# A hand-ordered attention and expert kernel: two cleared tiles fall away, and three weight splits change places at the end of attention

## The chip, the cores and the metric

The kernel runs on one core of a Trainium2 chip. The metric is the device time of one execution in microseconds (us); lower is better. Five engines take part, each with a program of its own that it works off in order: TensorE (PE in the profile, with its weight loads as PEld), VectorE (DVE), ScalarE (ACT), GpSimd (POOL) and SyncE (SP, which here only issues DMAs). GpSimd issues the gathers and scatters, which are indirect DMAs.

## The reference, cut to what matters

```python
# attention: 8 batches x 8 heads x 576 tokens, head size 64; k and v are averaged over groups of 8 tokens
k_p = k.reshape(B, H, 72, 8, D).mean(axis=3);  v_p = v.reshape(B, H, 72, 8, D).mean(axis=3)
attn = softmax((1 / sqrt(D)) * q @ k_p^T)
x = attn @ v_p                      # rows of 512 values, one for each of 8 * 576 = 4608 tokens
# experts: 8 of them, 512 -> 1024 -> 512; each token goes to one
logits = x @ w_gate;  local = sigmoid(x @ w_local)
# in each batch, token by token:
e = argmax(logits[s]) if s == 0 or local[s] < 0.5 else the expert of the token before
out[s] = softmax(logits[s])[e] * (relu(x[s] @ w1[e]) @ w2[e])
```

## The kernel before

**Attention** runs in 20 units, five to each of four pairs of batches (units 0 to 4 are pair 0, 15 to 19 pair 3). A unit takes 128 rows of queries of one or two tokens each, makes scores (`sc`), their maximum and difference (`mx`, `sb`, VectorE) and exponentials (`ex`, ScalarE), transposes them (`T0`, `T1`, `T2` on TensorE; `T0c` to `T2c` copy the result out on ScalarE), multiplies with the values (`v0`, `v1`, `v2` on TensorE, line 568; `v0c` to `v2c` copy out into `osb` on ScalarE), and scales: `fr` makes the reciprocals `rr` (line 585, VectorE), `fs` scales and sums the logits (`lgx`, line 590, and `lg`, VectorE), `fp` and `fd` scale the rows `xs` (line 606; both halves on GpSimd, or one on VectorE after `.d`) and send them to `x_rows` in DRAM.

**Routing** follows each pair in the steps `rA` (lines 624 to 639, VectorE), `rT0` to `rT2` (transposes into the small PSUM tiles `tp`), `rS0` to `rS2` (scans, line 653, VectorE), `rE`, `rL`, `rO`, `rR`, `rV` (lines 687 to 693, VectorE) and `rP`. It ends in nine scatters (`s`, line 707, GpSimd), which write each token's number into the list of its expert, `ids`.

**Weights.** After pair 1 the kernel chooses the expert with the most tokens so far and loads its weights (`w1`, `w2`). A float32 weight is used as a high and a low part. `p1:c` and `p2:c` split a piece of 128x1024: ScalarE writes the high part, and then a second engine subtracts it from the raw weights, which gives the low part. With `.d` that engine is VectorE, without it GpSimd:

```python
def split2(src, c, eng):
    s = slice(2 * c, 2 * c + 2)
    nc.scalar.copy(out=W2[0][:, s, :], in_=src)
    eng.tensor_tensor(out=W2[1][:, s, :], in0=src, in1=W2[0][:, s, :].bitcast(F32), op=ALU.subtract)
```

**First blocks.** `il` loads the token numbers of a block of 256 tokens of that expert (`idm`). `ga` turns them to integers (`idr`, line 292, VectorE), clears the tile `qt` that the rows go to (line 261, GpSimd), and issues two gathers from `x_rows` (line 265). Both blocks hold tokens of pairs 0 and 1 alone; a list entry past these rows is left out by the gather's bound. `X0` and `X1` transpose the gathered rows on TensorE (line 277), `X0c` and `X1c` copy and split them (line 284 on ScalarE, line 285 on VectorE). `L1` is the first layer (lines 322 and 324), `h0` and `h1` its results' way out of PSUM (lines 329 to 335; `h0` on ScalarE and then VectorE, line 330), `L2` the second layer (line 349).

**Order.** Nothing is scheduled by a planner. Three lists of steps are written out by hand (`PLAN` for attention, `PLAN_B` for the first two blocks and the last routing, `PLAN_C` for what follows), and each step puts its instructions on its engines in the order of the list, so that the list is at once the order within every engine. A loop over the other blocks follows; in it TensorE is busy almost all the time. TensorE's products use PSUM tiles with few buffers: `tp` has two, `op` has two, `hp` has three; the routing's transposes and those of attention share `tp`. `vt_in` and `kt` hold raw weights (three and two buffers), `qt` has four buffers.

Of the kernel before, what the change touches and what calls it, by code (L numbers as in the profile page):

```python
# [78 lines left out]
vc:19 v2c:12 ch:0 vm.a:22 fr:12 v0:11 v0c:11 sb:14 vc:20 T0:13 lk:14 v1:11 T0c:13 s:0 s:0 v1c:11 T1:13 v2:11 rR:1 er:0  # L79
T2:13 rV:1 vm.a:18 s:0 sc:15 T1c:13 rP:1 ex:14 T2c:13 vl:19 lq:17 w2:1 fp:12 lq:18 lq:16 v2c:11 vt:18 kc:15 v0:13 fr:11  # L80
vm.a:19 T0:14 mx:15 vd:19 vc:18 T0c:14 s:0 fp:11 w1:3 vl:20 sb:15 vd:20 T1:14 vt:22 v1:13 w1:2 T1c:14 vc:22 vl:18
fd.p:12 s:0 fd:11 fs:11 lv:23 vd:18 vm.a:21 sc:17 fs:12 vt:21 s:0 kp:14 ex:15 s:0 s:0 v0c:13 p2:1 v1c:13 v2:13
s:0 mx:17 sb:17 vc:21 v2c:13 p1.d:3 T0:15 w2:0 v0:14 fr:13 T0c:15 lq:19 vl:21 s:0 T1:15 v0c:14 s:0 fp.d:13 kc:14 T2:15
T1c:15 v1:14 v0:15 fs:13 v1c:14 fd:13 sc:16 fr:14 vd:21 vp.d:23 w1:1 T2c:15 ex:17 s:0 p1:2 fs:14 T0:17 v0c:15 fp:14
w1:0 T1:17 v1:15 vl:22 T0c:17 mx:16 T1c:17 v2:15 fd.p:14 T2:17 v1c:15 sb:16 il:0 vt:23 v0:17 vm.a:23 rA:2 vc:23 T2c:17
sc:18 v2c:15 ex:16 fr:15 T0:16 vd:22 mx:18 rT0:2 vl:23 vd:23 rS0:2 v1:17 T0c:16 T1:16 v0c:17 sb:18 v2:17 fp:15 v1c:17
T1c:16 T2:16 rT1:2 fd.p:15 p2:0 ga:0 fs:15 p1.d:0 v2c:17 fr:17 fp:17 v0:16 rS1:2 T2c:16 sc:19 ex:18 rT2:2 mx:19 v0c:16
rS2:2 v1:16 v1c:16 v2:16 rE:2 sb:19 v2c:16 T0:18 T0c:18 T1:18 rL:2 T2:18 T1c:18 fr:16 fs:17 ex:19 il:1 fd.p:17 fp:16
rO:2 fd:16 v0:18 rR:2 ga:1 T2c:18 fs:16 p1.d:1 X0:0 v0c:18 X0c:0 T0:19 v1:18 v1c:18 T0c:19 v2:18 X1:0 v2c:18 T1:19
rV:2 v0:19 fr:18 X1c:0 T1c:19 v1:19 v0c:19 fs:18 v1c:19  # L90
""")
PLAN_B = plan("""
# [13 lines left out]
def moe_attention(ctx: ExitStack, tc: tile.TileContext, q, q_st, k, v, v_st, w_gate, w1, w2, out):  # L106
    nc = tc.nc
# [149 lines left out]

    def rows_gather(i, xg, rows=None):
        row_numbers(idrs[i], idms[i])
        if rows:  # L260
            nc.gpsimd.memset(xg, 0.0)
        for h in range(2):
            off = bass.IndirectOffsetOnAxis(ap=idrs[i][:, h:h + 1], axis=0)
            if rows:
                nc.gpsimd.indirect_dma_start(out=xg[:, h, :], out_offset=None, in_=x_rows[0:rows], in_offset=off,
                                             bounds_check=rows - 1, oob_is_err=False)
            else:
                nc.gpsimd.indirect_dma_start(out=xg[:, h, :], out_offset=None, in_=x_rows[0:NT + 1], in_offset=off)
# [22 lines left out]
    def row_numbers(out, m):  # L291
        nc.vector.tensor_copy(out=out, in_=m[:, :, 0])  # L292
# [60 lines left out]
    with ExitStack() as actx:  # L353
# [405 lines left out]
        qg, qT, kg, vg, sc, att, fin, rw, tr2, vl = {}, {}, {}, {}, {}, {}, {}, {}, {}, {}  # L759
        first1, first2, lgs, fr = {}, {}, {}, {}  # L760
        reg = {}

        xg = xt = xs = xq = sp = None
# [9 lines left out]
        def do(name, n):  # L773
# [86 lines left out]
            elif op == "ga":  # L860
                xgs[n] = ld.tile([P, 2, D], F32, name="qt", bufs=4)
                rows_gather(n, xgs[n], 4 * S)
            elif op in ("X0", "X1"):
                xtp[n, op] = rows_turn(int(op[1]), xgs[n])
# [38 lines left out]
            elif op == "g1":  # L903
                xgs["n"] = ld.tile([P, 2, D], F32, name="qt", bufs=4)
                rows_gather(NS, xgs["n"])
            elif op in ("Y0", "Y1"):
                xt = xts[NS - 1]
# [370 lines left out]
```

## Time and profile before

| | us |
|---|---|
| median of 3 runs | 612.84 |
| lowest, highest | 612.37, 613.87 |
| the profiled execution | 618.07 |
| its span, first to last instruction | 615.5 |

The profiled execution has its own time; it is 5.2 us above the median of the runs without a profile, and 2.6 us of it lie outside the span. In its rows a start is counted from the span's start. A row of a timeline gives start, duration, engine, line, operation, output and inputs with shape, how many instructions are merged in it, and in brackets how long the engine sat idle just before and what ended the wait.

### The profile page before, as it was taken

The page shows a single profiled execution, that of the slowest core. Times are in us where ns is not written, and L with a number is a line of the kernel's source. Part 1 is how long each engine was busy: PE and PEld are TensorE (multiplying, and loading weights), DVE is VectorE, ACT ScalarE, POOL GpSimd, SP SyncE. Part 2 cuts the span into 40 slices and gives each one's busy share as a digit, 9 for nine tenths or more (in the row PEclk, how much of TensorE's full clock was granted, in tenths as well). Part 3 has the DMA queues.
Part 4 walks back from the last instruction along what each step waited for, and adds up shares of the span by engine and source line. Part 5 has one row for each costly group of instructions (what it writes and reads, how often), then busy time and mean ns, then how long its engine had stood idle before and what let it go on. Part 6 is the DMA issues. An engine that isn't in the chain of part 4 may idle for free. (4 is left out here: it accounts for less than half of the span.)

```text
span 615.5 us, 14456 instructions
## 1 busy us (share of the span) xinstructions
PE 593.8 (96%) x3392; PEld 512.7 (83%) x3393; DVE 412.6 (67%) x976; ACT 318.5 (52%) x732; POOL 281.9 (46%) x524
## 2 busy tenths in 40 slices
PE   8999999998999999999999999999999999999991
PEld 7998988987878888888888888888888888888881
DVE  7998898998866433643893585798536585634680
ACT  2777777965433223433662474668334473433561
POOL 6596776766475234232243426154152332331351
PEclk9999999997999999999999999999999999999997
DMA  8998983975102763422483457487743275223313
GB/s 345 358 390 296 358 290 108 332 166 169 56 1 98 229 235 115 130 79 91 118 325 104 146 186 289 125 333 221 269 123 107 102 274 186 92 80 101 114 40 91
DMA packets 62272, 111.94 MB, mean 182 GB/s; under 512 B 13730, under 2 KB 34210, under 8 KB 62244
## 3 DMA queue, kind: packets, MB, share of 16 engines
q1 hardware_dynamic: 53732, 89.54, 43.4%
q0 software_dynamic: 8512, 22.07, 10.9%
q8 instruction: 13, 0.21, 0.2%
q14 instruction: 15, 0.12, 0.1%
HBM read 81.88 MB, written 31.80 MB: 185 GB/s over the span
## 5 line engine op out<-in xcount | busy, mean ns | idle before, releaser
L322 PE MATMUL hp<-x,w1h 128*128 128x512 f32 x364 | 130.6, 399 | 0.5 <-DVE x L316 0.4
L349 PE MATMUL o_ps<-w2h,ht_h 128*128 128x512 f32 x312 | 122.8, 393 | 0.0
L349 PE MATMUL o_ps<-w2l,ht_h 128*128 128x512 f32 x312 | 122.0, 391 | 0.6 <-DVE w2l L178 0.5
L324 PE MATMUL hp<-x,w1l 128*128 128x256 f32 x364 | 102.1, 281 | 0.0
L330 DVE TENSOR_TENSOR hs<-hp,hs 128x256 f32<-128x256 f32 x91 | 37.7, 421 | 80.1 <-ACT hs L329 70.7
L349 PE MATMUL o_ps<-w2h,ht_l 128*128 128x512 f32 x312 | 87.6, 390 | 0.0
L322 PEld LDWEIGHTS hp<-x,w1h 128*128 128x128 f32 x364 | 68.4, 188 | 17.7 <-issue 0.8
L1107 POOL TENSOR_TENSOR zf<-m_e,ob 128x1 f32<-128x1 f32 x42 | 15.7, 375 | 128.8 <-ACT ob L1095 76.3
L568 PE MATMUL op<-vaug,aT 128*128 128x148 f32 (+4 forms) x448 | 67.4, 310 | 2.2 <-ACT osb L370 2.1
L324 PEld LDWEIGHTS hp<-x,w1l 128*128 128x128 f32 x364 | 68.7, 189 | 0.8
L349 PEld LDWEIGHTS o_ps<-w2l,ht_h 128*128 128x128 f32 x312 | 58.6, 188 | 12.9 <-DVE w2l L178 1.5
L349 PEld LDWEIGHTS o_ps<-w2h,ht_l 128*128 128x128 f32 x312 | 58.6, 188 | 12.5
L349 PEld LDWEIGHTS o_ps<-w2h,ht_h 128*128 128x128 f32 x312 | 58.6, 188 | 12.4
L334 ACT ACTIVATE ht_h<-hs 128x256 fp32r<-128x256 f32 x136 | 57.1, 421 | 22.4 <-DVE hs L330 14.7
L329 ACT COPY hs<-hp 128x256 f32<-128x256 f32 x91 | 33.5, 370 | 64.6 <-PE hp L324 56.6
L568 PEld LDWEIGHTS op<-vaug,aT 128*128 128x128 f32 (+1 forms) x448 | 61.1, 181 | 6.0 <-ACT osb L370 3.1
L335 DVE SCALAR_TENSOR_TENSOR ht_l<-hs,ht_h 128x256 fp32r<-128x256 f32 x136 | 57.3, 423 | 5.9 <-ACT ht_h L334 5.4
L1095 ACT ACTIVATE ob<-o_ps,m_a 128x512 f32<-128x512 f32 x40 | 27.4, 685 | 54.9 <-PE o_ps L349 54.9
L1108 POOL DMA_INDIRECT out<-ob,m_e x42 | 45.7, 1087 | 19.9 <-issue 18.5
L1106 POOL TENSOR_TENSOR m_e<-m_i,zi 128x1 int32<-128x1 int32 x42 | 12.5, 297 | 81.4 <-DVE m_i L292 75.5
L707 POOL DMA_INDIRECT ids<-pm,pos x36 | 38.7, 1076 | 17.3 <-DVE pos L702 8.2
L299 POOL DMA_INDIRECT vt_in<-x_rows,idk x40 | 39.8, 995 | 11.0 <-issue 9.2
(257 smaller groups left out, 1178.3 us busy)
## 6 DMA issues: line engine op xcount, KB each, us to landing
raw<-in_moe_w SPq DMA_DIRECT2D x48, 512.0 KB
xd<-vt_in SPq DMA_DIRECT2D x20, 512.0 KB
vt_in<-xd SPq DMA_DIRECT2D x80, 128.0 KB
kk<-in_k SPq DMA_DIRECT2D x16, 576.0 KB
qt<-in_q SPq DMA_DIRECT2D x16, 512.0 KB
vt_in<-in_v SPq DMA_DIRECT2D x16, 512.0 KB
x_rows<-xs SPq DMA_DIRECT2D x16, 512.0 KB
vt_in<-in_v_st SPq DMA_DIRECT2D x8, 256.0 KB
```

What stands on the lines that cost most here:

```text
L299: nc.gpsimd.indirect_dma_start(out=xg[:, h, :], out_offset=None, in_=x_rows[0:NT + 1], in_offset=bass.IndirectOffsetOnAxis(ap=idk[:, h:h + ...
L322: nc.tensor.matmul(out=ps, lhsT=W1[0][:, kk, f * P:(f + 1) * P], rhs=xt[:, kk].rearrange("p i n -> p (i n)"), start=(kk == 0), stop=False, ...
L324: nc.tensor.matmul(out=ps[:, 0:2 * P], lhsT=W1[1][:, kk, f * P:(f + 1) * P], rhs=xt[:, kk, 0, :], start=False, stop=(kk == KD - 1), skip_g ...
L329: nc.scalar.copy(out=hb[:, 0, :], in_=ps[:, 2 * P:])
L330: nc.vector.tensor_tensor(out=hb[:, 1, :], in0=ps[:, 0:2 * P], in1=hb[:, 0, :], op=ALU.add)
L334: nc.scalar.activation(out=ht[0][:, f, :], in_=hb, func=AF.Relu)
L335: nc.vector.scalar_tensor_tensor(out=ht[1][:, f, :], in0=hb, scalar=0.0, in1=ht[0][:, f, :].bitcast(F32), op0=ALU.max, op1=ALU.subtract)
L349: nc.tensor.matmul(out=to[h], lhsT=ht[i][:, kk, h * P:(h + 1) * P], rhs=W2[j][:, kk, :], start=(n == 0), stop=(n == 3 * KF - 1))
L568: nc.tensor.matmul(out=out, lhsT=lhs, rhs=rhs if len(out.shape) == 3 else rhs.rearrange("p s x -> p (s x)"), start=all(x[0] != n for x in ...
L707: ins = nc.gpsimd.indirect_dma_start(out=ids.rearrange("t m w -> (t m) w"), out_offset=bass.IndirectOffsetOnAxis(ap=pos[:, u:u + 1], axis= ...
L1095: nc.scalar.activation(out=ob[:, h, :], in_=o_ps[h], func=AF.Copy, scale=m_a[:, h, 1:2])
L1108: return nc.gpsimd.indirect_dma_start(out=outv, out_offset=bass.IndirectOffsetOnAxis(ap=m_e[h][:, 0:1], axis=0), in_=ob[:, h, :], in_offse ...
```

## The change

Two things are changed. `rows_gather` no longer clears the tile of gathered rows before the two gathers of `ga` (a row that the gather leaves out then holds what the buffer held before, old queries). And three steps of `PLAN` move: `p2:1` (a split of GpSimd) from between `v0c:13` and `v1c:13` to behind the scatter that follows `ex:17`, so that four more scatters stand ahead of it and `p1:2`, also GpSimd's, follows it at once; `p2:0` (GpSimd) from ahead of `ga:0` to behind `ga:1`; `p1.d:0` (a split of VectorE) from behind `fs:15` to behind `sb:19`, past the routing's second and third scan. With each split its copy on ScalarE moves too.

```diff
-fd.p:12 s:0 fd:11 fs:11 lv:23 vd:18 vm.a:21 sc:17 fs:12 vt:21 s:0 kp:14 ex:15 s:0 s:0 v0c:13 p2:1 v1c:13 v2:13
+fd.p:12 s:0 fd:11 fs:11 lv:23 vd:18 vm.a:21 sc:17 fs:12 vt:21 s:0 kp:14 ex:15 s:0 s:0 v0c:13 v1c:13 v2:13
 s:0 mx:17 sb:17 vc:21 v2c:13 p1.d:3 T0:15 w2:0 v0:14 fr:13 T0c:15 lq:19 vl:21 s:0 T1:15 v0c:14 s:0 fp.d:13 kc:14 T2:15
-T1c:15 v1:14 v0:15 fs:13 v1c:14 fd:13 sc:16 fr:14 vd:21 vp.d:23 w1:1 T2c:15 ex:17 s:0 p1:2 fs:14 T0:17 v0c:15 fp:14
+T1c:15 v1:14 v0:15 fs:13 v1c:14 fd:13 sc:16 fr:14 vd:21 vp.d:23 w1:1 T2c:15 ex:17 s:0 p2:1 p1:2 fs:14 T0:17 v0c:15 fp:14
 w1:0 T1:17 v1:15 vl:22 T0c:17 mx:16 T1c:17 v2:15 fd.p:14 T2:17 v1c:15 sb:16 il:0 vt:23 v0:17 vm.a:23 rA:2 vc:23 T2c:17
 sc:18 v2c:15 ex:16 fr:15 T0:16 vd:22 mx:18 rT0:2 vl:23 vd:23 rS0:2 v1:17 T0c:16 T1:16 v0c:17 sb:18 v2:17 fp:15 v1c:17
-T1c:16 T2:16 rT1:2 fd.p:15 p2:0 ga:0 fs:15 p1.d:0 v2c:17 fr:17 fp:17 v0:16 rS1:2 T2c:16 sc:19 ex:18 rT2:2 mx:19 v0c:16
-rS2:2 v1:16 v1c:16 v2:16 rE:2 sb:19 v2c:16 T0:18 T0c:18 T1:18 rL:2 T2:18 T1c:18 fr:16 fs:17 ex:19 il:1 fd.p:17 fp:16
-rO:2 fd:16 v0:18 rR:2 ga:1 T2c:18 fs:16 p1.d:1 X0:0 v0c:18 X0c:0 T0:19 v1:18 v1c:18 T0c:19 v2:18 X1:0 v2c:18 T1:19
+T1c:16 T2:16 rT1:2 fd.p:15 ga:0 fs:15 v2c:17 fr:17 fp:17 v0:16 rS1:2 T2c:16 sc:19 ex:18 rT2:2 mx:19 v0c:16
+rS2:2 v1:16 v1c:16 v2:16 rE:2 sb:19 p1.d:0 v2c:16 T0:18 T0c:18 T1:18 rL:2 T2:18 T1c:18 fr:16 fs:17 ex:19 il:1 fd.p:17 fp:16
+rO:2 fd:16 v0:18 rR:2 ga:1 p2:0 T2c:18 fs:16 p1.d:1 X0:0 v0c:18 X0c:0 T0:19 v1:18 v1c:18 T0c:19 v2:18 X1:0 v2c:18 T1:19
 rV:2 v0:19 fr:18 X1c:0 T1c:19 v1:19 v0c:19 fs:18 v1c:19
...
         row_numbers(idrs[i], idms[i])
-        if rows:
-            nc.gpsimd.memset(xg, 0.0)
         for h in range(2):
```

## Rows read from the trace of the kernel before

**Rows 1.** The page: busy time, share of the span and instructions of each engine.

```profile
PE 593.8 (96%) x3392; PEld 512.7 (83%) x3393; DVE 412.6 (67%) x976; ACT 318.5 (52%) x732; POOL 281.9 (46%) x524
```

**Rows 2.** Stretches (the second begins where v1:16 ends): length, each engine's busy us, clock.

```profile
112.00:136.30 24.30, 22.90 (x181) 20.90 (x179) 23.67 (x57) 18.79 (x48) 19.10 (x22) 1.00 0.88 243
140.39:143.84 3.45, 1.68 (x12) 1.23 (x11) 3.42 (x8) 1.97 (x6) 2.50 (x2) 0.96 0.16 23
143.84:150.20 6.36, 6.36 (x28) 5.84 (x29) 5.95 (x13) 2.92 (x6) 5.10 (x6) 0.50 0.60 216
...
155.87:161.32 5.45, 5.38 (x36) 4.34 (x32) 4.52 (x23) 1.17 (x5) 0.71 (x2) 1.00 0.00 1
```

**Rows 3.** VectorE's timeline up to the second block's numbers and its split, in order.

```profile
119.69 2.81 DVE L173 TENSOR_TENSOR w1l<-kt,w1h 128x1024 fp32r<-128x1024 f32 x1
...
129.27 1.02 DVE L625 TENSOR_TENSOR sh<-lg,ml 128x72 f32<-128x72 f32 x1
...
137.34 2.88 DVE L292 CAST idr<-idm 128x2 int32<-128x2 f32 x1 [1.06 <-DMA idm<-ids]
139.23 0.98 DVE L590 TENSOR_TENSOR lgx<-osb,rr 128x144 f32<-128x144 f32 x1
...
140.59 1.22 DVE L173 TENSOR_TENSOR w1l<-kt,w1h 128x1024 fp32r<-128x1024 f32 x1
...
144.36 1.82 DVE L585 TENSOR_SCALAR rr<-osb 128x16 f32<-128x16 f32 x1
...
148.32 0.23 DVE L292 CAST idr<-idm 128x2 int32<-128x2 f32 x1
...
149.34 1.22 DVE L173 TENSOR_TENSOR w1l<-kt,w1h 128x1024 fp32r<-128x1024 f32 x1 [0.20 <-ACT w1h L172]
```

**Rows 4.** GpSimd's timeline in the same stretch: splits, clearing, gathers, row scaling.

```profile
119.04 2.37 POOL L178 TENSOR_TENSOR w2l<-vt_in,w2h 128x1024 fp32r<-128x1024 f32 x1
...
127.26 2.36 POOL L173 TENSOR_TENSOR w1l<-kt,w1h 128x1024 fp32r<-128x1024 f32 x1
...
136.93 2.37 POOL L178 TENSOR_TENSOR w2l<-vt_in,w2h 128x1024 fp32r<-128x1024 f32 x1 [1.92 <-ACT w2h L177]
139.23 0.96 POOL L261 MEMSET qt<- 128x1024 f32 x1
141.03 1.73 POOL L265 DMA_INDIRECT qt<-x_rows,idr  x1 [0.84 <-POOL qt L261]
...
144.09 2.05 POOL L606 TENSOR_TENSOR xs<-osb,rr 128x512 f32<-128x512 f32 x2
...
149.30 1.04 POOL L265 DMA_INDIRECT qt<-x_rows,idr  x1 [0.77 <-POOL qt L261]
```

**Rows 5.** TensorE's timeline: the first block's first transposes, X0:0.

```profile
150.44 0.67 PE L277 MATMUL tp<-ident,qt 128*128 128x128 f32 x4
```

**Rows 6.** ScalarE's timeline: a split's copy, the routing's exponential, the exponentials ex:19.

```profile
136.75 1.05 ACT L172 CAST w1h<-kt 128x1024 fp32r<-128x1024 f32 x1
...
141.35 0.26 ACT L657 ACTIVATE pe<-sh 128x72 f32<-128x72 f32 x1
...
147.53 0.68 ACT L510 ACTIVATE at<-ap 128x576 f32<-128x576 f32 x1 [1.95 <-PE tp L526]
```

**Rows 7.** VectorE's timeline from X0c:0 to the first layer's first result, in order.

```profile
151.76 0.69 DVE L285 TENSOR_TENSOR x<-tp,x 128x512 fp32r<-128x512 f32 x1 [1.19 <-ACT x L284]
...
152.96 0.23 DVE L690 TENSOR_TENSOR pe<-pe,oh 128x72 f32<-128x72 f32 x1
...
154.19 0.17 DVE L585 TENSOR_SCALAR rr<-osb 128x16 f32<-128x16 f32 x1 [0.32 <-ACT osb L370]
...
154.65 0.69 DVE L285 TENSOR_TENSOR x<-tp,x 128x512 fp32r<-128x512 f32 x1
...
156.37 0.17 DVE L585 TENSOR_SCALAR rr<-osb 128x8 f32<-128x8 f32 x1 [0.38 <-ACT osb L370]
...
160.85 0.75 DVE L330 TENSOR_TENSOR hs<-hp,hs 128x256 f32<-128x256 f32 x2
```

## The prediction

> **What bounds the kernel now.** I read the page first: TensorE is busy for 96% of the span [rows 1], so a change gains only where TensorE stands, or runs slowly, near the moved steps. The table of stretches finds that place [rows 2]. From 140.39, where v1:16 ends, TensorE does 1.68 us of work in 3.45, so it stands for 1.77. Right after, from 143.84 to 150.20, it is busy throughout, but at a granted clock of 0.50, which is 1.2 GHz in place of 2.4. From 155.87, where the first layer begins, it hardly stands again (5.38 of 5.45). Next I asked who keeps TensorE waiting, in the chain of waits: `T0:18` and `T1:18` wait for VectorE's scans of the routing (they share the two `tp` tiles). So VectorE's timeline is the one to follow. It is busy for 23.67 of 24.30 us before 136.3 [rows 2], and its busy time holds hidden waits: a cast of 256 numbers takes 2.88 us where the same cast later takes 0.23, a `rr` of 16 columns takes 1.82, a split takes 2.81 where another takes 1.22 [rows 3]. Beside each stands a GpSimd instruction [rows 4]: the split of 2.81 us ends 1.09 after GpSimd's split (121.41), and 1.22 of work from 121.29 fills that out; the cast ends at 140.22, with the clearing (140.19); `rr` ends at 146.18, with the row scaling (146.14). So a VectorE instruction of these kinds stands until GpSimd's running one is over, and after 137.34 not even the border between two GpSimd instructions let it in. VectorE's order then sets the pace up to line 330 at 160.85 [rows 7], which frees the first `hp` tile, just as TensorE needs it at about 161.3. What VectorE gains by then, the kernel gains; behind it the lists are in fixed order and TensorE is full, so I carry the gain to the end one for one.
>
> **The change part by part.**
>
> *`p2:1` behind the scatters.* The split of `p1.d:3` at 119.69 no longer meets GpSimd's at 119.04: 2.81 - 1.22 = 1.59 us for VectorE. But now two GpSimd splits stand in one piece, 2 x 2.37 ending near 129.6 as the second does now (127.26 + 2.36) [rows 4]. Line 625, 1.59 us sooner at 127.7, meets the second and is let go at 129.6 to 130.2; now it ends at 130.29 [rows 3]. Left over: 0.1 to 0.7. If a `lgx` meets the first split instead, VectorE loses up to 2.37 and the edit is worth 1.59 - 2.37 = -0.8. I take +0.25. The scatters come 2.4 us sooner, and for them the load of `idm` waits: the 1.06 us that VectorE stands for `idm` at 137.34 goes (bounds 0 and 1.06; I take it all, since less than half of 2.4 is needed).
>
> *No clearing, and `p2:0` behind `ga:1`, first half.* Cast and `lgx` take from 137.34 to 140.21 and, with nothing beside them, 0.23 and some 0.3 (estimated; 0.98 at most): 1.7 to 2.3 us less, I take 2.3. With the 1.06, VectorE is past `lgx` at 140.2 - 3.4 = 136.8. The clearing (0.96, and 0.84 before the gather starts) is saved on GpSimd as well; it counts through VectorE alone, as the gathered rows are needed only at X0:0, 7 us later.
>
> *`p1.d:0` behind `sb:19`.* Its 1.22 us no longer stand ahead of the scans. TensorE's wait for `tp` goes: after v1:16 (140.39, unchanged, as TensorE works without a gap before it) v2:16, `T0:18` and `T1:18` follow at once. But the split is not free in its new place. Its copy on ScalarE (1.05 [rows 6]) now queues behind the copy of v1:16's result and the exponential of `rE`, which ends at 141.6 now and, being 0.26 long, at 140.65 at the earliest; I take 141.2, between the two. So the copy ends at 142.2, the split at 143.4, while VectorE was ready at about 140.8: of the 3.4 us some 2.5 are lost again. The next instruction, the `rr` of 1.82 us, starts at 143.4 in place of 144.36. The row scaling beside it (144.09) needs only the gathers out, and these leave 4 us sooner; it is over before, so `rr` takes some 0.2: 143.6 against 146.18, 2.6 sooner (0.9 if the row scaling still meets it). A further 0.4 I leave for `fp:16`, which now falls beside `lgx` and a scan. So the cast of `ga:1` comes 2.2 us sooner, at 146.1.
>
> *TensorE in the meantime.* Without the 1.77 us of idle I expect the clock to stay at 2.4 GHz: 6.36 us at half clock are 3.2 at full. Together 4.9; since `rO` needs VectorE, I count 4.4: X0:0 at 146.0 in place of 150.44 [rows 5].
>
> *`p2:0` behind `ga:1`, second half.* Its copy on ScalarE is covered: `ex:19` waits 1.95 us there for TensorE [rows 6], and without that cover it would cost 1.05. On VectorE, X0c:0 starts at 151.76 after 1.19 of idle, so VectorE was ready at 150.57, which is 2.25 after the cast; the idle was TensorE's half clock. New: 146.1 + 2.25 = 148.35, 3.4 sooner [rows 7]. But GpSimd goes from the cast (done 146.35) through two gathers and into the split. A gather took 1.73 where a VectorE split was already running (141.03, in the split of 140.59), and 1.04 where the split began just after it (149.30 and 149.34) [rows 3, 4]. The second gather will now be issued with `p1.d:1` running; two gathers, with some 0.3 between them, are 2.4 to 3.1, I take 3.1: the split runs from 149.4 to 151.8. Line 690 stands 1.20 behind X0c:0, at 149.55, and reads two tiles like line 625, which was held: it waits until 151.8, 2.25 lost. Then X1c:0, 2.89 behind X0c:0 less the 0.32 for which `rr` waited on ScalarE: 148.35 + 2.57 + 2.25 = 153.2 against 154.65, 1.45 sooner. The next `rr` no longer waits 0.38 for ScalarE. At line 330: 1.45 + 0.38 + 0.25 = 2.1 us. TensorE starts L1:0 behind X1c:0 at 153.9, 2.0 sooner, and so agrees.
>
> The sum against the profiled execution: 618.07 - 2.1 = 616.0, span 613.4; against the median 612.84 - 2.1 = **610.7 us**.
>
> A page of the Trainium skill would move one term. "SBUF — State Buffer", section "Who interferes with whom", infers that a `tensor_tensor` on VectorE does not hold up a gather's descriptors, as it takes only the read half of the port pair that the two engines share. The gather of 1.73 us does not agree, the one of 1.04 us does. By the page the sum would be 0.7 better, 610.0.
>
> **The rivals.**
>
> *The late split is not in the way* (0.17). If `p2:0` runs while VectorE is in instructions that read PSUM, or VectorE reaches X1c:0 ahead of it, the 2.25 are not lost: 612.84 - 4.3 = 608.5. For it: the two lie within 0.2 us of each other at 149.5. Against it: the split is 2.37 long and `rr` of `fr:18` would meet it next.
>
> *Gathers are not stretched* (0.07). GpSimd issues the second gather 0.7 sooner: 610.0. The row of 1.04 is for it, that of 1.73 against.
>
> *The clock falls again, ahead of the first layer* (0.14): slower. TensorE has work until about 151.8 and then stands until 153.9. Between 140.39 and 143.84 it was 1.77 us of idle that went before the fall to 1.2 GHz. If these 2.1 us do the same, a stretch like the 6.36 costs 3.2 us, on instructions that nothing hides: 612.84 - 2.1 + 3.2 = 613.9. [...] Against it: the work on both sides is dense here, and the idle there was in pieces between small transposes.
>
> *The gain is used up on the way* (0.10): the two joined splits hold VectorE 0.8 longer than before, and the clock falls as before at 144, since the routing's products of 16 columns still stand there: 612.84 - 2.1 + 0.8 + 1 = 612.5 (the 1 is what is left of 3.2 when VectorE's lost 2.25 lie beside it).
>
> **How the numbers follow.** The forecast has 0.52. Its own spread is about 1 us each way (the 0.1 to 0.7, the 0.9 to 2.6 at `rr`, half the lock). A difference under 0.3%, 1.84 us, can hardly be told from none; the line lies at 611.0, so of its 0.52 I give 0.31 to faster, 0.20 to the same and 0.01 to slower. The late split out of the way gives 0.17 to faster, unstretched gathers 0.06 and 0.01 to the same, the clock 0.02 to the same and 0.12 to slower, the used-up gain 0.08 to the same and 0.02 to slower. Faster 0.54, same 0.31, slower 0.15. The range is 608.2 (all of 4.3 and the best of the early edit) to 613.5 (most of the clock's case left out). The likeliest case alone is 609.7 to 611.7.
>
> **What the changed profile would show.** The cast of `ga:0` takes under 0.5 us without waiting for `idm`; `T0:18` waits for nothing; no stretch between 140 and 150 at a clock of 0.50; a VectorE wait of a microsecond ahead of the split of `p1.d:0`; X0:0 about 4 us sooner; then line 690 or an `rr` near 149.5 stretched to 2 us beside GpSimd's split, and TensorE idle ahead of L1:0. Wrong would make it: a clock still at 0.50 there, a split of GpSimd that costs VectorE nothing, or a L1:0 that comes sooner while `hp` is still late at line 330.

## The result, and the profile after

The changed kernel takes 617.89 us (median of 10 runs, 615.35 to 622.13) against 613.29 (10 runs, 611.29 to 613.88) for the kernel before, measured beside it. The ratio is 1.0082, 95% interval [1.0064, 1.01]: slower by 0.8%, where 610.7 was forecast. Three single executions in the sets below took 1193, 1515 and 2078 us and are in no ratio. The profiled execution took 618.28 with a span of 615.8, so here it lies beside its median.

On the page, the line that answers [rows 1] shows TensorE still at 96%:

```profile
PE 591.7 (96%) x3392; PEld 512.0 (83%) x3393; DVE 414.2 (67%) x976; ACT 319.2 (52%) x732; POOL 277.5 (45%) x523
```

The table of stretches (columns as in [rows 2]) puts the loss some 8 us ahead of the stretch that I had worked on:

```profile
130.00:134.00 4.00, 0.60 (x3) 0.60 (x4) 3.90 (x9) 0.98 (x2) 0.28 (x1) 0.94 0.87 267
134.00:136.00 2.00, 2.00 (x10) 2.00 (x10) 1.76 (x13) 0.36 (x2) 0.00 (x0) 0.50 0.15 53
136.00:138.00 2.00, 2.00 (x15) 1.80 (x13) 0.79 (x3) 0.00 (x0) 1.87 (x2) 0.76 0.03 1
138.00:144.00 6.00, 6.00 (x53) 5.44 (x52) 4.60 (x13) 4.86 (x12) 2.23 (x3) 1.00 0.30 103
144.00:150.00 6.00, 6.00 (x47) 5.64 (x45) 4.54 (x11) 4.53 (x9) 3.09 (x3) 1.00 0.46 163
...
156.00:164.00 8.00, 5.78 (x33) 4.47 (x34) 7.38 (x29) 1.30 (x5) 2.33 (x7) 1.00 0.21 85
```

TensorE works 0.60 of 4 us from 130 to 134, and then runs at a granted clock of 0.50 (1.2 GHz) before it comes back to 2.4. From 138 to 150 it is 1.00, where the profile of before showed 0.50 from 143.84 on. VectorE's timeline says what TensorE stood for; the lines from 140.67 on answer to [rows 3] and [rows 7]:

```profile
119.76 1.22 DVE L173 TENSOR_TENSOR w1l<-kt,w1h 128x1024 fp32r<-128x1024 f32 x1
...
124.52 5.86 DVE L588 TENSOR_TENSOR lgx<-osb,rr 128x72 f32<-128x72 f32 x1
...
137.34 1.42 DVE L493 TENSOR_REDUCE mx<-sp 128x12 f32<-128x864 f32 x2 [1.21 <-PE sp L472]
...
140.67 0.15 DVE L290 CAST idr<-idm 128x2 int32<-128x2 f32 x1
...
147.10 1.23 DVE L173 TENSOR_TENSOR w1l<-kt,w1h 128x1024 fp32r<-128x1024 f32 x1 [1.35 <-ACT w1h L172]
148.25 0.17 DVE L583 TENSOR_SCALAR rr<-osb 128x16 f32<-128x16 f32 x1
...
151.40 1.22 DVE L173 TENSOR_TENSOR w1l<-kt,w1h 128x1024 fp32r<-128x1024 f32 x1
152.54 0.68 DVE L283 TENSOR_TENSOR x<-tp,x 128x512 fp32r<-128x512 f32 x1
...
154.39 2.89 DVE L690 TENSOR_TENSOR pm<-pv,sm 128x9 f32<-128x9 f32 x1 [0.17 <-DVE pv L689]
...
163.32 0.75 DVE L328 TENSOR_TENSOR hs<-hp,hs 128x256 f32<-128x256 f32 x2
```

(Lines behind 262 are two lower than in the kernel before.) GpSimd's timeline beside it answers to [rows 4]:

```profile
124.47 2.37 POOL L178 TENSOR_TENSOR w2l<-vt_in,w2h 128x1024 fp32r<-128x1024 f32 x1
126.79 2.35 POOL L173 TENSOR_TENSOR w1l<-kt,w1h 128x1024 fp32r<-128x1024 f32 x1
129.11 1.17 POOL L604 TENSOR_TENSOR xs<-osb,rr 128x256 f32<-128x256 f32 x2
...
151.56 1.98 POOL L263 DMA_INDIRECT qt<-x_rows,idr  x1 [1.58 <-DVE lg L591]
153.84 1.00 POOL L263 DMA_INDIRECT qt<-x_rows,idr  x1 [0.30 <-issue]
154.87 2.38 POOL L178 TENSOR_TENSOR w2l<-vt_in,w2h 128x1024 fp32r<-128x1024 f32 x1
```

And TensorE's timeline shows its three waits, with X0:0 of [rows 5] between them:

```profile
133.40 3.90 PE L472 MATMUL sp<-kdz,qt 128*128 128x144 f32 x16 [4.38 <-DVE ap L496]
...
150.49 0.67 PE L275 MATMUL tp<-ident,qt 128*128 128x128 f32 x4
...
158.32 0.51 PE L320 MATMUL hp<-x,w1h 128*128 128x512 f32 x1 [1.43 <-DVE x L283]
...
163.79 0.50 PE L320 MATMUL hp<-x,w1h 128*128 128x512 f32 x1 [0.79 <-DVE hs L328]
```

`lgx` of `fs:14`, 72 columns wide, began 0.05 us after GpSimd's split and ended at 130.38, with the row scaling (130.28): it stood through two splits and two scalings of GpSimd, some 5.6 us, since the same instruction takes 0.23 unheld. TensorE stood 4.38 us for the difference `ap`, which VectorE makes behind `lgx`. The second hold is the one that I had forecast, behind `ga:1`.

### The profile page after: what moved, and what is told of

Its sections match the earlier page's. It is cut to its first block, busy times and chain, and to the rows that moved or that the text cites. A ratio compares the mean times of both kernels' runs of the same rounds, so it can differ in the third digit from the quotient of the medians.

```text
span 615.8 us, 14456 instructions
## 1 busy us (share of the span) xinstructions
PE 591.7 (96%) x3392; PEld 512.0 (83%) x3393; DVE 414.2 (67%) x976; ACT 319.2 (52%) x732; POOL 277.5 (45%) x523
## 3 DMA queue, kind: packets, MB, share of 16 engines
HBM read 81.88 MB, written 31.80 MB: 185 GB/s over the span
## 4 chain that ended last, share of the span: by engine, by line
PE 88%; DVE 5%; DMA 3%; ACT 1%; issue 1%; POOLq 0%; POOL 0%; SPq 0%; DVEq 0%; ACTq 0%
PE o_ps L347 35%; PE hp L320 13%; PE hp L322 7%; PE op L566 6%; PE tp L320 5%; PE hp L981 4%; PE sp L472 4%; PE tp L322 2%; PE rt L320 2%; PE tp L524 2%; DMA vt_in<-in_v_st 2%; DMA kk<-in_k 1%; PE rt L755 1%; PE rt L322 1%; DVE lgx L588 1%
## 5 line engine op out<-in xcount | busy, mean ns | idle before, releaser
L566 PE MATMUL op<-vaug,aT 128*128 128x148 f32 (+4 forms) x448 | 65.9, 306 | 0.7 <-ACT osb L368 0.6
L705 POOL DMA_INDIRECT ids<-pm,pos x36 | 37.3, 1036 | 14.9 <-DVE pos L700 8.3
```

The lines of the kernel that those rows point to most:

```text
L566: nc.tensor.matmul(out=out, lhsT=lhs, rhs=rhs if len(out.shape) == 3 else rhs.rearrange("p s x -> p (s x)"), start=all(x[0] != n for x in ...
L705: ins = nc.gpsimd.indirect_dma_start(out=ids.rearrange("t m w -> (t m) w"), out_offset=bass.IndirectOffsetOnAxis(ap=pos[:, u:u + 1], axis= ...
```

## The experiments

To place the time I read four marks in each trace: the start of VectorE's split of `p1.d:3` near 119.7, and from there to X0:0, to the first product of L1 and to the first result at line 330 (a start minus a start). From line 330 to TensorE's last product thirteen of the seventeen traces need 439.7 to 440.3 us, so among them what is won or lost at line 330 arrives at the end one for one, within 0.6. The other four need 441.0 to 441.8: the profile of [rows 1], and three of the kernels that were run on a chip where before took 615.2 (the first two with `fs:14` ahead, and the one with `p2:1` back and `p2:0` in L1).

Each mark is from one execution, which can lie off its kernel's median. The profile of the change with `p2:1` back is its quickest run (611.95, median 614.06), and so is that of the kernel without the clearing and with `p1.d:0` moved (611.45; its others go up to 615.57) and the first of `p2:0` subtracted in L1 (610.19, median 613.08).

| kernel | X0:0 | L1 | line 330 | ratio, interval |
|---|---|---|---|---|
| before, profile of [rows 1] to [rows 7] | 30.75 | 36.18 | 41.16 | |
| before again | 27.09 | 32.53 | 37.50 | 1.0003 [0.9993, 1.0014] |
| changed kernel | 30.73 | 36.17 | 43.56 | 1.0082 [1.0064, 1.01] |
| changed kernel again | 31.38 | 36.82 | 44.21 | 1.0099 [1.0079, 1.0119] |
| `p2:1` alone moved | 33.18 | 38.62 | 43.59 | 1.0091 [1.0074, 1.0107] |
| change with `p2:1` back | 25.63 | 31.07 | 38.46 | 1.0025 [1.0013, 1.0037] |
| change, scatter between the splits | 26.36 | 31.80 | 39.16 | 1.0033 [1.0012, 1.0054] |
| no clearing alone | 26.99 | 32.43 | 37.40 | 0.9992 [0.9982, 1.0001] |
| `p1.d:0` alone moved | 27.18 | 33.74 | 38.71 | 1.0014 [0.9997, 1.0031] |
| `p2:0` alone moved | 25.21 | 31.22 | 38.26 | 1.0002 [0.9992, 1.0013] |
| no clearing, `p1.d:0` moved | 27.29 | 32.73 | 37.69 | 1.0018 [1.0002, 1.0034] |
| change, `fs:14` ahead | 31.90 | 37.34 | 44.70 | 1.0105 [1.0066, 1.0144] |
| change, `fs:14` ahead, `p2:0` in L1 | 26.88 | 32.31 | 37.29 | 1.0053 [1.0024, 1.0082] |
| change, `fs:14` ahead, again | 25.51 | 30.95 | 38.33 | 1.0064 [1.004, 1.0089] |
| change, `p2:1` back, `p2:0` in L1 | 25.78 | 31.22 | 36.19 | 0.9954 [0.9929, 0.9979] |
| `p2:0` subtracted by VectorE in L1 | 25.39 | 30.84 | 35.80 | 0.9954 [0.9927, 0.998] |
| the same, again | 25.26 | 30.70 | 35.67 | 0.997 [0.9957, 0.9983] |

**The kernel before once more.** No edit; the question was what its profile looks like in another execution.

> The kernel before, unchanged, for a second profile of it. Theory P (the profile I read was not an ordinary execution: 618.07 us against a median of 613.3): a span near 610.5 us, and the fall of the clock to 0.50 at 143.84 to 150.20, which I counted as a gain to be had, is missing or shorter. Rival: the fall is there in every execution, and the missing 5 us lie elsewhere. Timed, 613.3 us, ratio 1.000 within 0.003 in either case.

The time is that of before (612.52 against 612.67), but the profile isn't the one I had read: line 330 comes 3.66 us sooner, and the span is 610.0 against 615.5. In its stretches the clock stays at 1.00:

```profile
140.00:144.00 4.00, 3.48 (x28) 2.83 (x27) 3.97 (x8) 2.36 (x6) 3.44 (x4) 1.00 0.33 88
144.00:150.00 6.00, 5.54 (x43) 5.23 (x39) 5.79 (x17) 3.76 (x8) 4.52 (x4) 1.00 0.65 235
```

and in VectorE's timeline the cast is over before GpSimd's split begins:

```profile
135.97 0.15 DVE L292 CAST idr<-idm 128x2 int32<-128x2 f32 x1
...
137.59 2.56 DVE L173 TENSOR_TENSOR w1l<-kt,w1h 128x1024 fp32r<-128x1024 f32 x1 [0.82 <-ACT w1h L172]
...
142.70 2.03 DVE L585 TENSOR_SCALAR rr<-osb 128x16 f32<-128x16 f32 x1
```

GpSimd's split and its clearing, from its own timeline:

```profile
136.69 2.37 POOL L178 TENSOR_TENSOR w2l<-vt_in,w2h 128x1024 fp32r<-128x1024 f32 x1 [1.91 <-ACT w2h L177]
139.00 0.96 POOL L261 MEMSET qt<- 128x1024 f32 x1
```

There is a hold here too, but it falls on the split of `p1.d:0` and costs 1.3, not 2.7; `rr` is held as in [rows 3]. The late load of `idm` (1.06 of wait in [rows 3]), the meeting of cast and split that follows from it, and the 6.36 us at half clock of [rows 2] belong to the execution I had read and weren't in this one, whose 612.57 lies at the median. The 618.07, 5.2 above the median, was the sign of it.

**The early edit alone, and the change without it.**

```diff
 # p2:1 alone moved, in the kernel before
-v0c:13 p2:1 v1c:13
+v0c:13 v1c:13
-ex:17 s:0 p1:2
+ex:17 s:0 p2:1 p1:2
```

The second kernel is the changed one with these two lines put back.

> The kernel before with p2:1 alone moved behind the scatters. Theory J (the joined GpSimd instructions hold VectorE's lgx for 5.9 us and all the loss comes from that): line 590 near 124.5 takes 5 to 6 us, TensorE stands for about 4 us near 130 and its clock falls there; 617 to 620 us. Theory L (the loss comes from the late split p2:0, which holds line 692 for 2.9 us): about as before, 613 to 614 us.

> The changed kernel with p2:1 back in its old place, the rest of the change kept. Theory J: no lgx above 2.4 us, TensorE's stand near 130 gone, 610 to 613 us, so at least 4 us under the changed kernel. Theory L: 616 to 618 us, as the late split stays. Of my prediction, if its second half was right: 611.

`p2:1` alone costs 0.91% (618.48), all that the change costs; with it put back 0.25% remains (614.06, over the 610 to 613 that theory J gave, under the 616 to 618 of theory L). With `p2:1` alone moved, `lgx` takes 5.81, beside the same run of GpSimd:

```profile
124.36 5.81 DVE L590 TENSOR_TENSOR lgx<-osb,rr 128x72 f32<-128x72 f32 x1
```

By the marks the early edit costs 43.56 - 38.46 = 5.1 us, and the rest of the change 38.46 - 37.50 = 0.96. The two don't simply add up: alone, the early edit costs 43.59 - 37.50 = 6.1. By the ratios it costs 0.57% on top of the rest (some 3.5 us), and 0.91% alone (5.6).

**A scatter between the two splits.** If `lgx` waits for a border between two GpSimd instructions, it was at one after 2.4 us. This kernel gives it a different border.

```diff
-ex:17 s:0 p2:1 p1:2
+ex:17 p2:1 s:0 p1:2
```

> The changed kernel with one scatter put between p2:1 and p1:2, so that GpSimd's two splits are not joined. Theory J, if VectorE is let in while GpSimd writes a scatter's descriptors: lgx waits for one split alone, up to 2.4 us, and 2 to 3.5 us of the loss are gone: 613 to 615.5 us. If a GpSimd queue that is never empty keeps VectorE out, whatever stands in it: 617 to 618, as changed. Theory L: 617 to 618.

VectorE's `lgx`, and GpSimd's timeline:

```profile
124.63 2.18 DVE L588 TENSOR_TENSOR lgx<-osb,rr 128x72 f32<-128x72 f32 x1
```

```profile
124.36 2.36 POOL L178 TENSOR_TENSOR w2l<-vt_in,w2h 128x1024 fp32r<-128x1024 f32 x1 [0.90 <-ACT w2h L177]
126.88 0.98 POOL L705 DMA_INDIRECT ids<-pm,pos  x1 [0.16 <-issue]
127.89 2.37 POOL L173 TENSOR_TENSOR w1l<-kt,w1h 128x1024 fp32r<-128x1024 f32 x1
```

It takes 614.5 us, as theory J had it for this case. Now `lgx` is let in as the first split ends (126.72), where GpSimd is idle for 0.16 before a scatter, and 4.4 of the 5.1 us at line 330 come back. ScalarE's copy of `p2:1` stays at its new place here, so it isn't the copy's move that costs. One split holds it for 2, two splits and two scalings without a gap for 5.6.

**The rest of the change, part by part.** The clearing left out alone (the rows that a gather leaves out then hold old queries); `p1.d:0` moved alone; `p2:0` moved alone; and the first two together. Each is the kernel before with the lines of that part of the diff.

```diff
 # p1.d:0 alone
-fs:15 p1.d:0 v2c:17
+fs:15 v2c:17
-sb:19 v2c:16
+sb:19 p1.d:0 v2c:16
 # p2:0 alone
-fd.p:15 p2:0 ga:0
+fd.p:15 ga:0
-ga:1 T2c:18
+ga:1 p2:0 T2c:18
```

> The kernel before without the two clearings (rows that a gather leaves out hold old queries then), nothing moved. Theory N (in an ordinary execution the cast of ga:0 runs ahead of GpSimd's split, and GpSimd has time to spare there): within 0.5 us of before, ratio 0.999 to 1.001. My prediction's pricing, where the clearing held the cast: 1 us faster.

> The kernel before with p1.d:0 alone moved behind sb:19. Theory F (the move is worth something by itself: VectorE's split no longer meets GpSimd's p2:0, which held it for 1.3 us, and the scans come sooner, so rr may miss the row scaling): 0.5 to 2 us faster. Rival W (in its new place it waits 1.35 us for ScalarE's copy, which eats what it wins): within 0.5 us of before.

> The kernel before with p2:0 alone moved behind ga:1, the clearings kept. Theory S (the late split holds VectorE at line 692 or at an rr near it for 2 to 3 us, and TensorE stands ahead of the first layer): 1 to 2.5 us slower, ratio 1.0015 to 1.004. Rival F2 (p1.d:0 is freed of the split and wins as much as is lost later): within 0.5 us.

> The kernel before without the clearings (rows that a gather leaves out hold old queries then) and with p1.d:0 moved; both GpSimd splits in their old places. This is the changed kernel without the two steps that theories J and S blame. By them: 0.5 to 2 us faster than before (611 to 612). If a loss is in the clearing's absence or in p1.d:0, it is slower than before.

None of them wins. Without the clearing: 612.24 against 612.81 (0.9992, theory N). `p1.d:0` alone gives 1.0014 [0.9997, 1.0031], not clear of the noise and no gain, so theory F missed; both together give 1.0018 [1.0002, 1.0034], where 0.5 to 2 us of gain were expected. With `p1.d:0` away, the next VectorE instruction, `rr` of `fr:17`, meets GpSimd's split in its place, and the routing of pair 2 keeps TensorE waiting. From VectorE's and TensorE's timelines of `p1.d:0` alone:

```profile
136.77 2.06 DVE L585 TENSOR_SCALAR rr<-osb 128x16 f32<-128x16 f32 x1
```

```profile
145.58 0.70 PE L682 MATMUL rt<-oh,lt 128*128 128x72 f32 x2 [1.31 <-DVE oh L675]
```

`p2:0` alone has the time of before (1.0002, rival F2) and shows the same exchange: X0:0 comes 1.9 us sooner than in before again, and line 330 comes 0.8 later, because a scaling of 9 columns at line 688 meets the split at its new place:

```profile
147.94 2.68 DVE L688 TENSOR_SCALAR sm<-sm 128x9 f32<-128x9 f32 x1
```

The hold moves, and isn't removed, as long as a split of GpSimd stands in the stretch that VectorE paces.

**No split of GpSimd in that stretch.** So I kept the copy of `p2:0` on ScalarE at its place and put the subtraction on VectorE into the first layer, in `PLAN_B`, where VectorE waits for TensorE. One kernel does this alone to the kernel before, one does it to the changed kernel with `p2:1` put back (its copy then stands behind `ga:1`).

```diff
+            elif op == "pc":
+                nc.scalar.copy(out=W2[0][:, 2 * n:2 * n + 2, :], in_=first2[n])
+            elif op == "ps":
+                c2 = slice(2 * n, 2 * n + 2)
+                nc.vector.tensor_tensor(out=W2[1][:, c2, :], in0=first2[n], in1=W2[0][:, c2, :].bitcast(F32), op=ALU.subtract)
...
-fd.p:15 p2:0 ga:0
+fd.p:15 pc:0 ga:0
...
-s:0 rE:3 X1:1
+s:0 rE:3 ps:0 X1:1
```

> The kernel before with p2:0's subtraction alone given to VectorE and put into the first layer (its copy on ScalarE stays). GpSimd's split at 136.7 is gone, so p1.d:0 is not held (2.56 to 1.22 us): line 330 comes 0.5 to 1.3 us sooner, 611.5 to 612.5 us. If rr of fr:16 still meets the row scaling and takes it back, within 0.3 us of before.

> The changed kernel with p2:1 back, and with the subtraction of p2:0 given to VectorE and put into the first layer, behind rE:3, where VectorE waits for ScalarE (its copy on ScalarE stays behind ga:1). If the late GpSimd split is what is left of the loss (line 692 held 2.9 us), line 330 comes 1 to 2.5 us sooner after the split of p1.d:3 than with p2:1 alone put back (38.46 us), and the time is 611.5 to 613, so at or under before. If the loss sits in p1.d:0's new place, it stays at 614.

Both come out faster, by the same ratio: 0.9954 [0.9927, 0.998] and 0.9954 [0.9929, 0.9979]. On this chip before itself takes 615.2 and scatters (612.82 to 620.41), though, and the second kernel was run on no other, so its gain rests on this one set. The first has line 330 at 35.80, 1.7 us sooner than before again: its split of `p1.d:0` takes 1.22 and its `rr` of `fr:16` 0.26. The second has it at 36.19, 2.3 sooner than with the late split.

**`fs:14` ahead of the splits.** If the hold of `lgx` is the whole cost of the early edit, then `lgx` at an earlier place removes it without `p2:1` going back. Only VectorE's order changes. The second kernel also has the subtraction of `p2:0` in the first layer.

```diff
-fr:14 vd:21 vp.d:23 w1:1 T2c:15 ex:17 s:0 p2:1 p1:2 fs:14 T0:17
+fr:14 fs:14 vd:21 vp.d:23 w1:1 T2c:15 ex:17 s:0 p2:1 p1:2 T0:17
```

> The changed kernel with fs:14 put ahead of vd:21 and vp.d:23 in the list: lgx then starts 0.7 us sooner on VectorE, ahead of GpSimd's joined splits, which stay as they are. Theory J (the loss comes from what VectorE happens to start during the joined GpSimd instructions): lgx takes 0.2 to 0.3 us; the next one that can be held is line 623 at about 127.5, and it is held until 129 to 130.3, 1 to 3 us in place of 5.9; 613 to 615.5 us, 2.5 to 5 under the changed kernel. Rival (the joined GpSimd splits cost as much wherever VectorE stands): 617 to 618.

> Both edits: fs:14 ahead, and p2:0's subtraction on VectorE in the first layer; p2:1 stays behind the scatters. If holds add up as told, 611.5 to 613.5 us, level with before or a little under; if the early meeting at line 623 costs more, 613.5 to 615.

Both missed: 621.88 (1.0105 [1.0066, 1.0144]) and 618.68 (1.0053 [1.0024, 1.0082]). `lgx` was no longer held (0.23), but something else stood. ScalarE's timeline of the first, and TensorE's:

```profile
125.81 0.53 ACT L368 COPY osb<-op 128x444 f32<-128x444 f32 x1 [6.17 <-issue]
```

```profile
126.39 2.68 PE L566 MATMUL op<-vaug,aT 128*128 128x148 f32 x8 [5.31 <-ACT osb L368]
```

ScalarE stood for 6.17 us, and the view names nothing that released it ("issue"). The semaphore events in the trace (a semaphore is the counter by which one engine tells another that it is done) say more: ScalarE waited for TensorE's, whose next four events came together, from 125.74 to 125.94, for products that are recorded as ended from 119.49 to 121.08. So the wait was for TensorE's word; what kept that back isn't shown. Was it the chip (before took 615.2 there) or this order? Three kernels on another chip were to tell:

> The changed kernel once more. My theory (lgx of unit 14 held through four GpSimd instructions): ratio 1.007 to 1.010 to before, lgx some 5.8 us, no wait of ScalarE near 119.6. The rival (the wait of ScalarE is of the chip, not of an order of steps): it shows the 6 us wait of ScalarE as well, and a ratio near 1.01 whatever lgx does.

> The changed kernel with fs:14 (two instructions of VectorE) ahead of vd:21, once more. My theory: lgx takes 0.3, ScalarE doesn't wait near 119.6, ratio 1.000 to 1.005. The rival (this order itself makes ScalarE wait): ratio 1.01 again, with the wait of 6 us ahead of osb and 5 us of TensorE. In the second case the hold of lgx isn't shown to be the whole of what p2:1 cost.

> The kernel before with the subtraction of p2:0 alone on VectorE in the first layer, once more. My theory (no split of GpSimd stands in the stretch that VectorE paces): ratio 0.994 to 0.998, line 330 some 1.7 us sooner than in before. The rival (its gain was that chip's): ratio 0.999 to 1.001.

The changed kernel is as slow as in its first runs (618.7, 1.0099), with `lgx` at 6.02 and no wait of ScalarE. The kernel with `fs:14` ahead is scattered: 12 runs from 612.1 to 619.97, five of them below 615 and seven above 616.7, ratio 1.0064 [1.004, 1.0089], above the 1.000 to 1.005 that my theory gave. Its profile is of a run of 613.84. In it ScalarE doesn't wait near 119.6, `lgx` takes 0.23, and line 330 stands at 38.33, as with `p2:1` put back (38.46). VectorE's and GpSimd's timelines of that run:

```profile
123.61 0.23 DVE L588 TENSOR_TENSOR lgx<-osb,rr 128x72 f32<-128x72 f32 x1
...
127.76 2.49 DVE L623 TENSOR_TENSOR sh<-lg,ml 128x72 f32<-128x72 f32 x1
```

```profile
126.65 2.37 POOL L173 TENSOR_TENSOR w1l<-kt,w1h 128x1024 fp32r<-128x1024 f32 x1
128.97 1.18 POOL L604 TENSOR_TENSOR xs<-osb,rr 128x256 f32<-128x256 f32 x2
```

Line 623 is held in place of `lgx`, as I had expected of the first try: through the second split and both scalings, to 130.25. That takes back what the split of `p1.d:3` gains. So in such a run the early edit costs nothing more at line 330 once `lgx` is out of the way. The order with `fs:14` ahead loses some 4 us again in about half of its runs, on this chip too. Whether they lose them to ScalarE's wait wasn't seen, as the one profile here fell on a quick run; the wait stands in one trace of this order, and a similar one (3.32 us, whose releaser the view doesn't name either) in the kernel that has `p2:0` in the first layer besides; there it stands ahead of the split of `p1.d:3`, which starts at 127.29 only, so the marks of the table don't show it. ScalarE's instructions are the same, in the same order, in the changed kernel, whose two profiles don't have it. Events of TensorE's semaphores that are over 0.15 us behind the recorded end of their product, or missing in the record, are 30 to 41 of 251 in the four traces of that chip and in the profile of [rows 1], and at most one in the other twelve. They are there with every order of steps, so they speak for the chip and the execution; what they come from stays open, and so does what slows the seven runs here.

The third kernel settles that the gain of `p2:0` subtracted by VectorE isn't an accident of one chip: 610.6 against 612.27, 0.997 [0.9957, 0.9983]. Its timeline of VectorE has the split of `p1.d:0` unheld, and from there to line 330 no instruction above 1.3 us:

```profile
137.70 1.23 DVE L173 TENSOR_TENSOR w1l<-kt,w1h 128x1024 fp32r<-128x1024 f32 x1 [0.82 <-ACT w1h L172]
...
155.38 0.75 DVE L330 TENSOR_TENSOR hs<-hp,hs 128x256 f32<-128x256 f32 x2
```

Its table of stretches has TensorE without a gap from 140 to 150 at full clock:

```profile
140.00:150.00 10.00, 10.00 (x89) 9.39 (x87) 8.89 (x27) 7.11 (x17) 6.08 (x10) 1.00 0.71 225
```

## Why the prediction was wrong

**`p2:1` behind the scatters, the step that failed.** It was taken at +0.25, with -0.8 "if a `lgx` meets the first split instead", a loss of at most one split, 2.37. The `lgx` did meet it, and it stood not through one but through four GpSimd instructions: 5.1 us at line 330, shown by `p2:1` alone, by `p2:1` put back, by the scatter between, and by the quick run with `fs:14` ahead. The 5.1 are the hold of 5.6, less the 1.4 that the split of `p1.d:3` gained as foreseen (1.22 at 119.76, against 2.66 with `p2:1` back), less 1.1 by which lines 623 and 624 are no longer held, and some 2 more. The largest piece of these that the trace shows is VectorE's wait of 1.21 for TensorE's scores (137.34), made at half clock behind the 4.38 us that TensorE stood; that part wasn't tried by itself. The rows had a warning: the cast of 2.88 in [rows 3] stood through a split and the clearing behind it in [rows 4], and I wrote that not even the border let it in, then priced the new pair of splits as if the border would. But they had the other case as well. Line 625 (129.27 to 130.29 in [rows 3]) stood through the end of a split and the first of two scalings, and was let in between the two, where GpSimd doesn't stand either (its timeline in before):

```profile
129.57 1.19 POOL L606 TENSOR_TENSOR xs<-osb,rr 128x256 f32<-128x256 f32 x2
```

It is so in all eleven traces in which that instruction meets the end of the second split, with `p2:1` at its old place or a scatter between. So a hold can last through a whole run of GpSimd, and doesn't always; what decides at which border VectorE is let in wasn't found.

**The gains that I counted weren't in the kernel, but in one execution.** Cast, first `lgx` and the wait for `idm` (2.3 and 1.06), the 1.77 of idle and the 3.2 of clock are nearly all absent from before again, whose time is the median's. The whole stretch to line 330 was 3.66 us longer in the profile that I read. I had noted that its time was 5.2 us above the median, and let the sum end at the median as if the excess lay elsewhere.

**The late half went as told, step by step.** VectorE waits 1.35 for ScalarE ahead of the split of `p1.d:0`, and wait and split take 2.57 (some 2.5 forecast); `rr` behind it takes 0.17 (0.2); `T0:18` waits for nothing; the cast takes 0.15; the clock is 1.00 to 150. A gather is stretched, to 1.98, by the split of `p1.d:1` (151.40), the late split of GpSimd runs 2.38, and VectorE loses 2.72 to it (2.25 forecast), only two instructions behind the line that I named. TensorE stands 1.43 + 0.79 = 2.2, though behind L1's first four products and not ahead of them (2.1). With `p2:1` put back, line 330 stands at 38.46; my sum, without the 0.25, put it at 158.75 + 0.25 - 119.69 = 39.3. The place is as forecast within 0.9, the gain isn't, since before has 37.5 and not 41.2.

**The clearing** was worth nothing by itself (0.9992), which I had only as a share of 2.3.

**The rivals.** *The gain is used up on the way* had the right place and direction (joined splits, a clock that falls) and 0.8 where 5.1 were due. *The clock falls again ahead of the first layer* had its condition, 2.2 us of idle, and the clock stayed at 1.00 from 156 to 164. But with the same wait (1.42) it did fall in two other traces. The tables of stretches of the kernel with a scatter between and of `fs:14` ahead, again:

```profile
156.00:158.00 2.00, 2.00 (x7) 1.69 (x7) 1.73 (x10) 0.12 (x1) 0.00 (x0) 0.50 0.00 0
```

```profile
154.00:156.00 2.00, 2.00 (x8) 1.65 (x7) 1.76 (x9) 0.37 (x1) 0.61 (x1) 0.50 0.00 0
```

So the rival's fall can come; that it spared the changed kernel's trace is luck. Its price of 3.2 isn't seen: line 330 stands at 39.16 and 38.33 in these two, against 38.46 without the fall, since VectorE sets the pace there. *The late split is not in the way* and *gathers are not stretched* fell: 2.89 at line 690, 1.98 at the gather. Carrying line 330 to the end one for one held within 0.6 us in thirteen traces; the profile that I started from is one of the four others.

By the marks the early edit is 5.1 + 0.25 off and the late half, by its start from the wrong execution, 0.96 + 1.85: 8.2 together. By the medians it is 4.6 + 2.1 = 6.7. The marks are each from one execution.

## What to carry to other kernels

Bound a hold by the whole run of instructions that the other engine has queued without a gap, not by the one that is running. The run is the worst case and not a rule, since one VectorE instruction stood through four here and another was let in at a border without a gap. Joining two long instructions of GpSimd cost VectorE 5.6, where the parted ones had cost 1.4 and 1.1. Before a stretch's idle time and clock are counted as gain, compare the profiled execution's own time with the median: where it is 0.8% above, the stretch may be that execution's alone. Where moved work only moves the hold, give it to the engine that was held, in a stretch where that engine waits: 0.3 to 0.5% here, from one subtraction.

## What the runs showed of the hardware

A VectorE instruction with both inputs in SBUF stood through four GpSimd instructions that followed each other without a gap (5.86, 5.81 and 6.02 us in three traces, 0.23 unheld). Its recorded start lay 0.05 and 0.11 us behind the first split's in two of them, and 0.11 ahead of it in the third (123.59 against 123.70), so the order of the recorded starts doesn't say who is held. With a scatter behind the first split, and 0.16 us of idle before it, the instruction was let in there (2.18); whether the idle piece did it or that it was a scatter wasn't tried apart. At another border without a gap, between two row scalings, VectorE was let in in eleven traces. I had expected a hold of at most one instruction.

In before again, VectorE's split of 2.56 ends at 140.15; with 1.22 of work it was let in at 138.93, as GpSimd's clearing (139.00) began. The Trainium skill ("SBUF — State Buffer", "Who interferes with whom") says that an instruction of VectorE with two SBUF inputs contends with a GpSimd instruction that reads SBUF, not with one that only writes it, and this row agrees. The same section's inference that such an instruction leaves a gather's descriptors alone doesn't: the gather beside VectorE's split took 1.98, the next one 1.00.
